# DMA transposes of q and k in three parts, ten x buffers and a new order, in a sliding-window attention with a gated feed-forward stage

## The chip, the core and the metric

The kernel runs on one core of one Trainium2 chip. The metric is device microseconds for one execution of the whole program. Of this kernel four runs are known: 302.01, 302.12, 302.18 and 303.75 us, median 302.15 us. A core has engines that each work through their own list of instructions in order and wait for each other by semaphores: PE (matrix products and transposes through the systolic array), DVE (vector), ACT (scalar functions), POOL (here it makes the masks' distances and issues loads that also convert f32 to bf16) and SP (here it issues stores and DMA transposes).

## The reference

There are 8 batches of 8 heads, 576 positions and 64 values per head. The first half is attention over a window of 128 positions back, with a linear bias per head; the second is a feed-forward stage with h * cos(h) between its two products.

```python
scores = scale * np.matmul(q, k.transpose(0, 1, 3, 2))      # scale = 1/8
bias = slopes[:, None, None] * (-np.abs(rel).astype(np.float32))[None, :, :]
mask = (rel >= 0) & (rel < window)                           # rel = i - j, window = 128
scores = np.where(mask, scores + bias[None], -1000000000.0)
attn = softmax of scores over j
x = (attn @ v), rows (batch, position), columns (head, value)   # 4608 x 512
h = x @ w_in                                                 # 512 -> 2048
out = (h * np.cos(h)) @ w_out                                # 2048 -> 512
```

## The kernel before

**Work.** The 4608 rows of x are 9 chunks of 512. A chunk's feed-forward stage is `moe1` (16 blocks of `w_in`; each block is 4 matmuls at L768, a cosine on ACT at L774 and a multiplication on DVE at L778 that writes g) and `moe2`, the second product (L909; chunk 0 has its own forms at L792 and L853). From chunk 1 on `moe2` computes seven products of half-sized blocks (P1 to P7) from sums of weights and of g; its `read` steps on ACT (L929) and DVE (L933) add them and write one of four output buffers `ob`, which `store` (L954) sends to memory. A buffer can be written again only when its last store has landed.

**Attention.** A batch is nine units: four head pairs for the first 256 positions (G = 0), four for the next 256 (G = 1), and a tail of 64 positions for all heads. For a unit PE computes scores (L538), ACT the exponential (L568), DVE the mask (L592), PE the product with v (L623, L626), DVE the division (`norm`, L664, or for two units at once L679), which writes x into a buffer of `xnat`. x must then be transposed into `xT`. For units that the next chunk needs, PE does it (`x_pe`, `x_pe_two`) and ACT or DVE copies; for others SP issues a DMA transpose (`x_dma`, L753; tails from `xtail`, L748). The buffers of `xnat` are used in turn, `n % NX`, so a `norm` must wait until the transpose that read its buffer NX units earlier has landed.

**q and k.** They are needed with the head's 64 values on partitions. Batches 0 and 1 (`BPE = 2`) are transposed on PE by `qk_transposes` (L481) into two PSUM banks at a time, and copied out by ACT (L498) and DVE (L499). Batches 2 to 7 are loaded by POOL (`load_nat`, L339, five loads each for q and k) into `qnat` and `knat`, two buffers each, and transposed by DMA into `qt` and `kt` (`dma_transposes`): one transfer of the first four blocks of 128 positions (L350) and one of the tail of 64 (L353), with one semaphore for both. Every score group of a batch waits for all of that batch's q and k. Loads of batch 3 wait for batch 2's transposes.

**Order.** The code describes operations with what they read and write (`op`), a modelled length `occ` and delay `lat`. POOL's operations keep the order of the code. For all others the order on each engine, and which of ACT and DVE takes an operation that both could do, come from a table of start times, `STARTS`, that was made beforehand and stands in the file in packed form. `schedule` sorts by it; `emit` turns the dependences into semaphore waits. So the engines' lists are fixed when the program is built, and an instruction whose input is late holds up all that stands behind it on its engine.

Of the kernel before, what the change touches and what calls it, by code (L numbers as in the profile page):

```python
# [14 lines left out]
B, H, S, D = 8, 8, 576, 64  # L15
NPAIR = H // 2
NBLK = 5
# [10 lines left out]


STARTS = (  # L30
    "c-pO24RBP|72cOXa(x5(I4W)~i!PU!n68h_l0Nn)ci$#JvTT>Qh5<sb{46Q06ag_HP0@nHLTijMGE9d;#FQ$-pI~Q%qT-BFY"
    "cW#GD1!*tv9_RN!730;7P7DBy<IjxyHU&ZC42Y0bI-l^obP<++_eaL+;Z(nNjm=Fn{E-hvv26ov#utlbwS5Rz**D4Fw`x*pT"
    "UBV^`+(7ocZasXYy75rdI*~@V_gyWw)jG2H!=pWYA@ZG2>cuRv5@Gp1~`N9uu;Y?k8>az8(mA2LG}y8DnmDmXKv07aJt#!dG"
    "b#T<xzIe5LQZkY(xYtI59Ro!-mSxEWTr8CvgIy<c2?HTnQ!iXs`~y*B9S7z<ffg|CyW=^i*+18UL~@&1aev~36X#RmzN9m|L"
    "h%0hq4uNR*Te9$uty#ng)CCAJ(4T>9B33!wc6NG+o_j|YGbpG$)WnW3t#QL$Tub(~45lmS~VkM;6q-!h#Xs|qVQ?F;LQ&eUp"
    "8dP`6COh6EW2X=jSr<AJSf!WD_3$c9A@paOklWGUCbu)g`n3Kfq;x`WXN7NEo9XHPj%$TXf$2T?3WgK8U-wWc7Ef8`=obc?T"
    "XdRv64G7j?$5+QSH3*~mT#-$tengJO$K#lWTGX>#O}1+GHZkZ>)346i3_dgP8=LJ&>7s7GRwBaQgT*zSE53MEB_DDr9FdU{j"
    "0GLyUkFNcXK9KdhEYTfeHf`XtJC40y$X@F>{5Wr`25iI#`jW$oV?0mv^OM)HOgq?(UWG-nmX$3IpGSee{AEwh;T)tLM6|t2E"
    "?<^rF9<=4>xF(cZWmu4#JYc(1aEe`APoOIExO=~M2<Q+^BAzSI1Rr?tim8eAXGfJHn5U{yu>`?oQfna`Ic1qF8NvYf3s(e1J"
    "DA4)zHOAc-M4Scrk@ldEN6xvebYB{>~Y^`Iq{>5y)cD(<lGW}FpS((2C2b>RuR@c2}eXYiJXwmKaXTl+vl7A+!oY|a=%_)*P"  # L40
    "1HKXG3(v8R+{ny#JW{7TY(&?nyMvD{TR8pHc=?!gxBV@-U7ku8d-gn%-%`Ma16?JZ*8Z&y2Qo{At=e8jL_*xu%105=FM=di@"
    "jnA99e}zUP+)|JRz6G;32H>^<Z&tiLW$^{JkqulP!<FHY1~6R>D^w!|49rxLW=oZAhLw>RNIUyQV5l|^S?>72F(5Tp&ca+RO"
    "TIM9f%Oc$|r_Oq5<DLw`+?>zZ#95XkRjvZL{s1_2gKXI(n4TJCXWtE|Mx_n;IHhIKu-KOmc^PQJU?OD)K9Q;Ot&+;HAAEsw{"
    "~b(%X+8w?`W&tC0X|K$U{kAOS0m19b#g<044~30(y59NS4iaiLd|gED*bkz0bHdWIUPUhZyV;AUs-f#PCRFuo5YHK4sv6LdH"
    "6iPdjP0quU7v>xX_T-dgW@hiCHiqh4%XQ1?Hrouv=hbPFsH7cI_(+8m%!ka%deDKXhpUNwK8$?;V6P;k=S8w%tF9wg(w}O+$"
    "z$Dq_^iHPsQ7Go;6^DyH|CI-o!ynzh!?oTJN00M>oNqItta{zsFyr;t+m1#*cYTQ98VNNA5Q+8OdlQnBROj(ZT9q=A@ne075"
    "M>%QM6sDr5DWGjNez{Vvdu`PXd8Q`&?z!e^5PN-wKg~1HS&NVV(LX{1#t(8>4cJlDlo?9)>F#(%W4ZW@hLIZxJ|oA)cR)Lv3"
    "<F^llvG{Gd_C(Kvb&$rr3E=HH8V<?->O<UkuU$#=l|_aB6=92KI@Q)N-(wu14tXeCo-=OUBt6>7rNeGe8;Ra*w5#<`%&uCKr"
    "eAypX`h9h&EAK~c-U&j$`Y5N-d6N)3D*e6{M_C!r&uRR?d3ZjME7nH7CExOhl&3M=F(SOd##QaFi?4ZrhFeM}Uw2T>+lcM=i"
    "#3)8@$FAy88Q$$!$Kumn`Q!wVC3yM4FG7yKAt{_wq-`bZb;3At!%8Z@ZDn<Q*8C-fG2+Ypcf-E)h$=;uom1q}LC~NV(QFaI#"  # L50
    "crKL`<eP+T#J3kY<K`ogQFi`VvFu>l2gsR|+H7;5*AOelH$&uvQ=5oPL#zr9@Ba(kZ#(i-5j^?*9ctAw*JB>=&7b2A4c$q*e"
    "9|4>FFa8F!Io(I-ukV-zGsZ}rXkI>?Z4Qvo$f7y=jUJe9C>Bm{%BO+u+hGvWTR6Hd=}jx88L$ihjqS;h}EZ{kw*BQgB0;>go"
    "+Z~h$Dp()Ho@T5#Ji8h;))5XtPm+VtErQ@yo{U#f`(Hd;)1)Jn67ZT$K2oHny~YP<4^}%R)lToeTI56?+ji_;qXIDAL5Apy*"
    "Q-9a6x#SRIN`_n}bfJ=lvxhv>BPJi<&vyY{I_B|}vBTw*Sj?OZn{1_eCV=wn7bXp7BqA)=k%WS$}6X<dd2=NX@8_{|JE0cRE"
    "Lgib!=#r6AdZHbQXc%NxK=MLXhTla=X7B1Cjpv-V8?xD-2`U(z1l}8-j7w9XtCyS()y_?pBqM=QP-#O-J%ZWOo<5VztWi#=k"
    "U_H_-lK_Egl3*3&ttpYEp2D^%Qdyme3Zy`{7ML`4p?6R$ZYOYukA>0GN>sZHqjEU^>Oo2rHw|2BP$IOIKDW}^R7(xM3<IoP-"
    "=9FDO{K3o{#DmnI@PPPhQ-T{OF=vD07_Nf9axVndqRQ}v!1Ph0P^mP6lip7XC#H@Xrr)&70i2HVM+m?zQLiedp<&j+O;VYmV"
    "`b%+ScKLXIjs?!$W^bi#+hN>c+_+kE~MM&pTdm|E{QT%KUQ<Z~lRoX3Z;-W}luZb-IYxMb0-Utq!q)(j>=dt<lGVP?>xeNBB"
    "0;p85<B#b%wKfG|<gINokgKw1W*7!0$#hu0aXc_XUm6v^pz;mFgzCFc6FAo4r3n<#Urzs6|Ez6XO8!@Qq@)HL~&#Foc>AE}*"
    "D=KDverp(TBRYj`RJiCqJy9=+60KZdWwhh`^Rg%@xwcuCmKe!nuS?N;@zh)MF5-Fdf<@>SKRUj<k7uqhLnhsOvSE}KmTj^*I"  # L60
    "{P<X*2P*$Fu4UuWLa(cBbK?o@8Hq?RSZY-Y+{k`$nrL)oBa}&1KmsWM6d+Y~234u~juR@BuQIzE7?oGO5!Nlp+qWJ_Gl*qGr"
    "Ah-Lw7z1>Zs}?S*&IRY?C}SvYAya4YTQk;cl|v)hfRIhp&&!n1cNwgFCJVU<op<HU&`N6BGPic29~x?(;kv!y!~eQ7Yu6F9z"
    "I%!_rUk$`Z_xojy7U-?OLhA0j+~U<Hy=+P}RcHA#;wojzpu!MiQAa_iiM9V_lT`_gGh|;!;sXmMZwmqa4IMU%gEI)J!N<F^{"
    "TskXRiAl^Q=E77`j&t)Eb;h$>NQ9H^t>hB4FklOV2P3iV^vBQ3@*drnkU8B`J^iisvIzPw>ii=A&)DQ%kjqsX?EZf)qfbE<v"
    "%t_ZM_D~lVgH`@98Dny#KeK28(mp>4xYc154)kq8c&s>bwMeKY>^#-=2^tM)@jr{zAh6AkhRI92efBiY0E05o{&>Cv5UU>9v"
    "3RJ<n1J6bGDOuSzoGDvW%;5^=P>5~Yp=U?Wm=P9(W)6)zl_+(A%WOV~H4@%F?QUx3_r2imWCu9pPkf&lJ#6$wB!+Pzoldeq&"
    "+iz$H9-$(Pu7LR&a(dk0l(UW"
)


# [150 lines left out]
def bass_alibi_sliding__then__act_gcu_kernel(  # L221
# [8 lines left out]
    with ExitStack() as ctx:  # L230
# [3 lines left out]
        R = Plan(nc, ctx)  # L234
        op = R.op
# [7 lines left out]
        T = {n: sb(f"wsum{n}", [128, HF, 256], F16) for n in (1, 2, 3, 4)}  # L243
        Sg = {n: sb(f"gsum{n}", [128, HF, 256], F16) for n in (1, 2, 4)}
        qB = {"q": sb("qrows", [128, 2, 1152]), "k": sb("krows", [128, 2, 1152])}
        nat = {w_: [sb(f"{w_}nat{i}", [128, NBLK, H, D]) for i in range(2)] for w_ in ("q", "k")}
# [5 lines left out]
        NP = 4  # L252
        P = [sb(f"p{i}", [128, 2, 512]) for i in range(NP)]
        Pt = [sb(f"ptail{i}", [128, 1088]) for i in range(2)]
        NX = 8
        xbuf = sb("xnat", [128, NX, 256])
        xnat = [xbuf[:, i, :] for i in range(NX)]
        xtl = [sb(f"xtail{i}", [64, 512]) for i in range(2)]
# [76 lines left out]
        def load_nat(which, src, b):  # L335
            fns = []
            for t in range(NBLK):
                rows = 128 if t < 4 else 64
                fns.append(lambda e, t=t, rows=rows: e.dma_start(  # L339
                    nat[which][b % 2][0:rows, t, :, :],  # L340
                    src[b, :, 128 * t:128 * t + rows, :].rearrange("h p d -> p h d")))

            op("pool", fns, r=[("tr", which, 0)] if b == 3 else [], w=[("nat", which, b % 2)],
               dma=f"ldn{which}{b % 2}", occ=4400, lat=4500)

        def dma_transposes(b):
            for which in ("q", "k"):
                t = tr[which][b % 2][:, :].rearrange("p (c k t) -> p c k t", c=NBLK, k=NPAIR)
                fns = [
                    lambda e, t=t, which=which: e.dma_start_transpose(  # L350
                        t[:, 0:4, :, :].rearrange("p c k t -> p (c k) t"),
                        nat[which][b % 2][:, 0:4, :, :].rearrange("p c h d -> p (c h d)")),
                    lambda e, t=t, which=which: e.dma_start_transpose(  # L353
                        t[:, 4, :, 0:64],
                        nat[which][b % 2][0:64, 4, :, :].rearrange("p h d -> p (h d)")),
                ]
                op("sp", fns, r=[("nat", which, b % 2)] + ([("ktail", b % 2)] if which == "k" else []),
                   w=[("tr", which, b % 2)], dma=f"tr{which}{b % 2}", occ=2500, lat=4300)

        def load_w_in(u):  # L360
            op("pool", [lambda e: e.dma_start(
# [141 lines left out]
        def tkeys(u):  # L503
            b, _, G = u
            keys = [("tr", w_, b % 2) for w_ in ("q", "k")] + [("ktail", b % 2)]
            if b < BPE:
                keys += [("tr", w_, b % 2, t0 + j0) for w_ in ("q", "k")
                         for t0, _, groups in PIECES[b] if not (G == 0 and t0)
                         for j0, _ in groups]
            return keys  # L510
# [554 lines left out]
        for c in range(NCH):  # L1065
            if c == 0:
                for i in range(NFC):
                    moe1_half(c, i // 8, i % 8, (OB + SB)[i] if i < 6 else (OB + SB)[i % 4])
                for half in range(2):
                    qk_transposes(1, "q", 0, half, SB[2:4])  # L1070
                    qk_transposes(1, "k", 0, half, SB[2:4])
                load_nat("q", q, 2)
                load_nat("k", k, 2)
            else:
                for fc in range(NFC):
                    moe1(c, fc, (UB + SB)[fc % 6] if done < len(every) else
                         (UB + SB)[(16 * c + fc) % 6])
            n = QUOTA[c] if c < len(QUOTA) else 0
            attention(every[done:done + n], c)
            done += n  # L1080
            while next_t < B and done >= 9 * (next_t - 1):
                load_v(next_t)
                if next_t < 4:
                    tail_zero(next_t)
                dma_transposes(next_t)
                next_t += 1
                if next_t < B:
                    load_nat("q", q, next_t)
                    load_nat("k", k, next_t)
            moe2(c)  # L1090
# [29 lines left out]
```

The softmax here doesn't subtract the row's maximum and nothing guards it: scores larger than these inputs give would overflow.

## Time and profile before

| | before |
|---|---|
| median of 4 runs | 302.15 us |
| profiled execution, its own time | 302.12 us |
| its span | 300.4 us |
| granted TensorE clock | 1.00 |
| PE busy | 291.4 us, 97% of the span |
| DVE, ACT, POOL busy | 240.5, 209.6 and 95.0 us |
| L768, first product of a chunk, in the chain | 36% of the span |
| L909, second product, in the chain | 34% of the span |
| DMA traffic | 38.09 MB, mean 127 GB/s |

The span is the time from the first to the last instruction of the program on the core. In a line of groups or of the timeline, PE, DVE, ACT, POOL are the engines, SPq is SP issuing, L followed by a number is the line of the kernel, and `out<-in` gives the buffers. What stands in brackets after a row is the idle time of the engine before it and what ended it; "issue" there means that the profile shows nothing that it waited for. PE's matmuls are pipelined, so the lengths of neighbouring rows overlap.

### The profile page before, as it was taken

Reading aid. Unit: us, or ns where it says so; the run is one execution under the profiler, and the core shown is the slowest. Engines: PE = TensorE matmul, PEld = TensorE weight load, DVE = VectorE, ACT = ScalarE, POOL = GpSimd, SP = SyncE. Lnnn points to the kernel's source line nnn. Section 1 sums busy time; section 2 is a strip of 40 time slices with the busy share of each in tenths; the row PEclk is TensorE's granted clock in tenths of the full one; section 3 lists DMA queues with packets and bytes.
Section 4 is the critical chain, followed back from the end, with each engine's and each line's share of the span. In section 5 each row is a group of like instructions: output and inputs, shape, how many; then the busy total and the mean of one; then the engine's idle time right before and its main releaser. Section 6 shows DMA issues by size and latency. Waiting matters only on the chain.

```text
span 300.4 us, 7105 instructions
## 1 busy us (share of the span) xinstructions
PE 291.4 (97%) x2905; PEld 200.6 (67%) x2925; DVE 240.5 (80%) x478; ACT 209.6 (70%) x300; POOL 95.0 (32%) x122
## 2 busy tenths in 40 slices
PE   7799999999999999999999999999999999999996
PEld 3568746547774578547888886568746855566685
DVE  4587678879978998899988889788978967685871
ACT  6787978398857788588768685778676945644432
POOL 7998230059955702760196004000000000000000
DMA  7999999999999999999999999932304111120033
GB/s 139 180 199 210 206 168 174 139 165 144 188 141 140 173 159 156 144 183 166 174 117 146 136 119 159 170 71 65 98 26 99 44 30 52 37 77 30 0 124 122
DMA packets 148352, 38.09 MB, mean 127 GB/s; under 512 B 133984, under 2 KB 147040, under 8 KB 148320
## 3 DMA queue, kind: packets, MB, share of 16 engines
q0 software_dynamic: 99344, 18.10, 78.0%
q1 hardware_dynamic: 48976, 19.54, 36.2%
q8 instruction: 23, 0.38, 0.5%
q14 instruction: 9, 0.07, 0.1%
HBM read 36.70 MB, written 9.44 MB: 154 GB/s over the span
## 4 chain that ended last, share of the span: by engine, by line
PE 93%; DMA 2%; DVE 1%; issue 1%; POOL 1%; ACT 0%; POOLq 0%; DVEq 0%; ACTq 0%
PE ps L768 36%; PE ps L909 34%; PE ps L792 5%; PE ps L853 5%; PE ps L538 5%; PE ps L623 3%; DMA krows<-in_k_dram 2%; PE ps L626 2%; PE ps L481 1%; PE ps L692 1%; PE ps L528 1%; PE ps L610 1%; PE ps L612 1%; DVE xnat L664 1%; POOL krows L310 0%
## 5 line engine op out<-in xcount | busy, mean ns | idle before, releaser
L768 PE MATMUL ps<-xT,w_inb 128*128 128x512 bf16 (+1 forms) x556 | 125.2, 354 | 0.7
L774 ACT ACTIVATE cos<-ps,halfpi 128x512 f32<-128x512 f32 x128 | 82.3, 686 | 46.3 <-PE ps L768 34.9
L778 DVE TENSOR_TENSOR gT<-ps,cos 128x512 f16<-128x512 f32 x128 | 83.0, 685 | 21.6 <-ACT cos L774 21.1
L768 PEld LDWEIGHTS ps<-xT,w_inb 128*128 128x128 bf16 x576 | 55.2, 98 | 39.7 <-DVE xnat L679 0.8
L568 ACT ACTIVATE p<-ps 128x768 bf16<-128x768 f32 (+1 forms) x64 | 55.6, 917 | 8.5 <-PE ps L538 7.6
L329 POOL DMA_DIRECT2D vp<-in_v_dram x40 | 34.0, 872 | 64.1 <-PE ps L626 50.5
L909 PE MATMUL ps<-wsum,gT 128*128 128x256 f16 x256 | 50.8, 273 | 0.4
L592 DVE TENSOR_TENSOR p<-p,emask 128x512 bf16<-128x512 bf16 (+2 forms) x88 | 39.0, 471 | 3.4 <-ACT p L568 3.0
L909 PE MATMUL ps<-w_outb,gT 128*128 128x256 f16 x256 | 39.7, 273 | 0.1
L909 PE MATMUL ps<-wsum,gsum 128*128 128x256 f16 x256 | 37.2, 273 | 0.1
L339 POOL DMA_DIRECT2D qnat<-in_q_dram x30 | 25.4, 897 | 20.6 <-DMA qt<-qnat 17.1
L909 PEld LDWEIGHTS ps<-wsum,gT 128*128 128x128 f16 x256 | 24.2, 98 | 9.1 <-DVE ob L933 0.8
L909 PEld LDWEIGHTS ps<-w_outb,gT 128*128 128x128 f16 x256 | 24.5, 98 | 8.4 <-ACT ob L929 0.3
L909 PEld LDWEIGHTS ps<-wsum,gsum 128*128 128x128 f16 x256 | 24.7, 98 | 4.6 <-ACT qrows L929 0.2
L339 POOL DMA_DIRECT2D knat<-in_k_dram x30 | 25.6, 927 | 3.3 <-issue 3.3
L909 PE MATMUL ps<-w_outb,gsum 128*128 128x256 f16 x128 | 26.1, 273 | 0.1
L679 DVE TENSOR_TENSOR xnat<-ps,rec 128x512 bf16<-128x512 f32 x28 | 19.3, 690 | 1.3
L929 ACT ACTIVATE qrows<-ps 128x512 f32<-128x512 f32 (+1 forms) x18 | 9.9, 552 | 14.2 <-PE ps L909 14.1
L538 PE MATMUL ps<-qt,kt 64*128 64x128 bf16 (+1 forms) x320 | 18.4, 239 | 0.5 <-issue 0.3
L623 PE MATMUL ps<-vp,p 128*128 128x65 bf16 x256 | 18.0, 193 | 0.8 <-DVE xT L740 0.4
L623 PEld LDWEIGHTS ps<-vp,p 128*128 128x128 bf16 x256 | 15.6, 97 | 3.9 <-issue 1.2
L626 PE MATMUL ps<-vp,p 128*128 128x65 bf16 x192 | 16.9, 193 | 0.0
(81 smaller groups left out, 333.3 us busy)
## 6 DMA issues: line engine op xcount, KB each, us to landing
out_dram<-ob SPq DMA_DIRECT2D x32, 256.0 KB, 4.2
vp<-in_v_dram POOLq DMA_DIRECT2D x32, 128.0 KB, 9.2
qnat<-in_q_dram POOLq DMA_DIRECT2D x24, 128.0 KB, 12.8
knat<-in_k_dram POOLq DMA_DIRECT2D x24, 128.0 KB, 17.3
w_inb<-in_moe_w_in_dram POOLq DMA_DIRECT2D x4, 512.0 KB, 10.8
w_outb<-in_moe_w_out_dram POOLq DMA_DIRECT2D x4, 512.0 KB, 22.2
out_dram<-ob SPq DMA_DIRECT2D x8, 128.0 KB, 1.7
qrows<-in_q_dram POOLq DMA_DIRECT2D x1, 576.0 KB, 15.5
```

Source lines behind the costliest of these rows:

```text
L329: op("pool", [lambda e, t=t, rows=rows: e.dma_start(vp[b % 2][0:rows, t, :, 0:64], v[b, :, 128 * t:128 * t + rows, :].rearrange("h p d -> ...
L339: fns.append(lambda e, t=t, rows=rows: e.dma_start(nat[which][b % 2][0:rows, t, :, :], src[b, :, 128 * t:128 * t + rows, :].rearrange("h p ...
L538: ins = e.matmul(ps[:, banks[x], c0:c1], keys_ap(b, x, pr, kc), query_ap(b, x, pr, qb, 128 * nb), start=not added, stop=True, skip_group_c ...
L568: op("act", lambda e: e.activation(P[i][:, :, 0:hi], src_[:, :, 0:hi], ACTF.Exp, scale=0.125), w=held + [("P", i)], occ=920 if G else 691, ...
L592: op("dve", lambda e, p=p, m=m: e.tensor_tensor(p, p, m, ALU.mult), r=[("P", i), ("EM", h0), ("EM", h1)], w=[("P", i)] if n != 1 else [("P ...
L623: ins = e.matmul(o, P[i][:, x, d0:d0 + 128], V[:, kc, h, 0:65], start=True, stop=not two)
L626: ins = e.matmul(o, P[i][:, x, p0:p0 + 128], V[:, kc - 1, h, 0:65], start=False, stop=True)
L679: op("dve", lambda e: e.tensor_tensor(o, U[:, :, :, 0:64], rv[:, :, :, None].broadcast_to([128, 2, 4, 64]), ALU.mult), r=[("rec", n // 2 % ...
L768: op("pe", lambda e, kc=kc, c0=c0: e.matmul(ps[:, bank, c0:c0 + n], w_in[:, kc, 128 * fc:128 * fc + 128], xT[:, kc, (r0 + c0) % XR:(r0 + c ...
L774: op("act", lambda e: e.activation(cosb[ci][:, :], ps[:, bank, :], ACTF.Sin, bias=halfpi[:, 0:1]), r=["halfpi"], w=[("B", bank), ("cos", c ...
L778: op("dve", lambda e: e.tensor_tensor(gT[gi][:, fc, :], ps[:, bank, :], cosb[ci][:, :], ALU.mult), r=[("cos", ci)], w=[("B", bank), ("g", ...
L909: op("pe", lambda e, t=t, fc=fc, bk=bk: e.matmul(ps[:, bk, 256 * t:256 * t + 256], lhs(fc, t), rhs(fc), start=first and fc == 0 and (last ...
```

## The change

- `NX`, the number of x buffers in `xnat`, goes from 8 to 10.
- `dma_transposes` issues three transfers for each of q and k: blocks 0 and 1, blocks 2 and 3, and the tail, each with a semaphore of its own, in the code's order k before q. For batches 2 to 7 that is 36 DMA transposes in place of 24.
- `tkeys`, the list of what a score group waits for, names parts: a unit with G = 0 needs the first part of q and k, one with G = 1 the second part of q and the first two of k, the tail unit the last of q and the last two of k.
- Loads of batch 3 wait for the second part of batch 2's transposes only.
- The PE transposes of batch 1's q go to the other pair of PSUM banks, those of its k stay.
- The modelled lengths of the transposes change, and the table of start times is a new one: order and choice of engine change throughout. In the new lists ACT and DVE share some copies differently, and on SP the parts of the transposes stand between stores and x transposes.

```diff
-        NX = 8
+        NX = 10
...
-            op("pool", fns, r=[("tr", which, 0)] if b == 3 else [], w=[("nat", which, b % 2)],
+            op("pool", fns, r=[("tr", which, 0, "p", 1)] if b == 3 else [], w=[("nat", which, b % 2)],
                dma=f"ldn{which}{b % 2}", occ=4400, lat=4500)
 
         def dma_transposes(b):
-            for which in ("q", "k"):
-                t = tr[which][b % 2][:, :].rearrange("p (c k t) -> p c k t", c=NBLK, k=NPAIR)
-                fns = [
-                    lambda e, t=t, which=which: e.dma_start_transpose(
-                        t[:, 0:4, :, :].rearrange("p c k t -> p (c k) t"),
-                        nat[which][b % 2][:, 0:4, :, :].rearrange("p c h d -> p (c h d)")),
-                    lambda e, t=t, which=which: e.dma_start_transpose(
-                        t[:, 4, :, 0:64],
-                        nat[which][b % 2][0:64, 4, :, :].rearrange("p h d -> p (h d)")),
-                ]
-                op("sp", fns, r=[("nat", which, b % 2)] + ([("ktail", b % 2)] if which == "k" else []),
-                   w=[("tr", which, b % 2)], dma=f"tr{which}{b % 2}", occ=2500, lat=4300)
+            for part, (c0, c1) in enumerate(((0, 2), (2, 4), (4, 5))):
+                for which in ("k", "q"):
+                    t = tr[which][b % 2][:, :].rearrange("p (c k t) -> p c k t", c=NBLK, k=NPAIR)
+                    src_ = nat[which][b % 2]
+                    if part < 2:
+                        o = t[:, c0:c1, :, :].rearrange("p c k t -> p (c k) t")
+                        i = src_[:, c0:c1, :, :].rearrange("p c h d -> p (c h d)")
+                    else:
+                        o = t[:, 4, :, 0:64]
+                        i = src_[0:64, 4, :, :].rearrange("p h d -> p (h d)")
+                    op("sp", [lambda e, o=o, i=i: e.dma_start_transpose(o, i)],
+                       r=[("nat", which, b % 2)] + ([("ktail", b % 2)] if which == "k" else []),
+                       w=[("tr", which, b % 2, "p", part)], dma=f"tr{which}{b % 2}{part}",
+                       occ=3150 if part < 2 else 1300, lat=1900 if part < 2 else 500)
...
             keys = [("tr", w_, b % 2) for w_ in ("q", "k")] + [("ktail", b % 2)]
+            parts = {"q": (0, 1, 2), "k": (0, 1, 2)}
+            if b >= BPE:
+                parts = {0: {"q": (0,), "k": (0,)}, 1: {"q": (1,), "k": (0, 1)},
+                         None: {"q": (2,), "k": (1, 2)}}[G]
+            keys += [("tr", w_, b % 2, "p", i) for w_ in ("q", "k") for i in parts[w_]]
...
-                    qk_transposes(1, "q", 0, half, SB[2:4])
+                    qk_transposes(1, "q", 0, half, SB[0:2])
                     qk_transposes(1, "k", 0, half, SB[2:4])
```

The lines of `STARTS` are left out of the diff; all of them change.

## The prediction

> **What bounds the kernel now.** I read the page's totals first, then the chain, then idle time by stretch, then the waits of PE, and only then the queue that the change rewrites (SP).
>
> ```profile
> span 300.4 us, 7105 instructions
> PE 291.4 (97%) x2905; PEld 200.6 (67%) x2925; DVE 240.5 (80%) x478; ACT 209.6 (70%) x300; POOL 95.0 (32%) x122
> PE 93%; DMA 2%; DVE 1%; issue 1%; POOL 1%; ACT 0%; POOLq 0%; DVEq 0%; ACTq 0%
> ```
>
> PE is busy for all but 9.0 us, and 93% of the chain is PE. The stretches say where the 9.0 us lie (first column the stretch, second its length, third PE's busy time):
>
> ```profile
> 0.00:5.00 5.00, 3.74 (x9) 1.20 (x9) 1.09 (x7) 2.45 (x5) 3.42 (x12) 1.00 0.52 134
> 5.00:10.00 5.00, 4.17 (x75) 2.77 (x76) 3.13 (x13) 4.17 (x10) 5.00 (x7) 1.00 1.22 164
> 10.00:15.00 5.00, 3.35 (x70) 2.40 (x70) 3.28 (x9) 4.03 (x6) 5.00 (x8) 1.00 1.79 181
> ...
> 30.00:40.00 10.00, 10.00 (x115) 6.82 (x113) 7.32 (x13) 8.68 (x14) 1.57 (x2) 1.00 1.29 204
> 40.00:50.00 10.00, 10.00 (x100) 5.49 (x99) 7.66 (x18) 7.78 (x10) 3.30 (x4) 1.00 2.36 166
> ...
> 175.00:200.00 25.00, 24.48 (x235) 15.17 (x236) 20.91 (x44) 17.61 (x26) 3.32 (x4) 1.00 1.02 141
> ...
> 275.00:300.40 25.40, 22.40 (x179) 17.34 (x179) 14.39 (x25) 9.83 (x19) 0.00 (x0) 1.00 0.22 73
> ```
>
> Up to 25 us PE idles 4.4 us, of which 1.3 us come before its first instruction; from 25 to 275 us it idles 1.6 us in all; the last stretch idles 3.0 us, nearly all of it the last eviction, store and landing. The waits of PE are short and, apart from those at the start, hardly there:
>
> ```profile
> PE ps L481 <- DMA krows<-in_k_dram: 0.7, 1, 0.7
> PE ps L730 <- DVE xnat L664: 0.6, 1, 0.6
> PE ps L623 <- DVE xT L740: 0.4, 1, 0.4
> PE ps L538 <- issue: 0.3, 1, 0.3
> ```
>
> The fourth is the one PE wait that the timeline puts on the transposes of q and k, at 178.4 us. In the timeline (start, length, engine, line, operation):
>
> ```profile
> 178.65 0.51 PE L538 MATMUL ps<-qt,kt 64*128 64x256 bf16 x8 [0.28 <-issue]
> ```
>
> Two more places of the timeline matter below: SP's queue from 120 us, and a row of DVE that needs a store to have landed.
>
> ```profile
> 120.39 4.89 SPq L350 DMA_TRANSPOSE qt<-qnat  x1
> 125.33 1.38 SPq L353 DMA_TRANSPOSE qt<-qnat  x1
> ...
> 130.57 0.61 SPq L954 DMA_DIRECT2D out_dram<-ob  x1
> ```
>
> ```profile
> 139.87 0.69 DVE L933 TENSOR_TENSOR ob<-ps,qrows 128x512 f32<-128x512 f32 x1
> ```
>
> **The change part by part.**
>
> *PE's own work.* Both programs hold the same 2,925 weight loads and matmuls; only their order differs. So the 291.4 us stay. One thing in the order has a price: entering a score group or a PE transpose from other work. Five L909 matmuls start at 200.81 and the score group after them at 201.45: 0.64 us where five steps of 0.109 make 0.545, so 0.10 us per entry. Before has 39 such entries, after 40: **+0.1 us**.
>
> *The start, up to 21 us.* The new order takes the bias and score matmuls of heads pair 2 out of the wait for the last k rows and puts them behind it. Step by step: the k rows land at 10.94 as before (POOL's order is unchanged), transposes run 10.98 to 11.66, bias and scores of pair 3 to 12.37 as before, then those of pair 2 (0.44 and 0.27) to 13.08, so the first L623 group starts at 13.1 against 12.76. Both copies of kt now stand on DVE, 0.87 us each, where ACT took one: 11.78 to 13.4, just in time. ACT then runs the exponentials of pair 3, pair 2 and two groups of 0.97 until 15.95, and the xT copy, two exponentials and another copy that follow reach to 18.5. DVE's masks (0.68 each, a 0.28 copy between) end at 17.9, so the next L623 group starts at 17.95 against 17.84, with 9 of the first L792 matmuls done instead of 11 (2 x 0.109). At the following L623 group DVE has one more mask ahead of the copy that it waits for: 20.7 against 20.39, with 15 L792 matmuls done against 16. That is 0.3 + 0.1: **+0.4 us**. Bounds: −0.6 if the waits of the second and third lines above (0.6 and 0.4) go and nothing replaces them but the 0.4; +1.0 if a further 0.6 us wait of the same kind comes. I take +0.4, since the chain of rows gives it.
>
> *Batch 1's PE transposes in two bank pairs.* They could spare waits for the copies out of one pair (0.87 to 0.88 us a copy). But from 30 to 50 us PE is busy 20.00 of 20.00 us: the L792 and L853 matmuls fill those waits. **0**; if that cover were gone, one copy, +0.9.
>
> *Ten x buffers.* No row of the waits shows DVE waiting for an xT transpose before it writes xnat. **0** directly; it lets the new SP order send x transposes later. A gain needs a wait that isn't there; a loss would be an x transpose that lands late, which belongs to SP's queue below.
>
> *DMA transposes in three parts.* The 12 of L350 (16 blocks, 4.9 to 6.7 us of SP while loads run, 2.1 when they don't) become 24 of 8 blocks; the 12 of L353 (1.3) stay. A half has no row: between an xnat transpose (2 blocks, 1.25) and the whole (6.7). I take half of a whole, 2.6 for the first after a quiet spell (4.89/2), 3.0 behind another. So SP issues 12 more, at least 0 and at most 12 x 1.3 = 16 us, on a queue that PE doesn't read. What it buys: a score group waits for its own parts. The 0.28 us wait at 178.4 is for the tail of batch 6's q, issued at 171.23. In the new order the first halves of q and k of batch 6 go out near 147 and 161; the wait goes: **−0.3 us**. The first group of batch 3 becomes the tighter one: its k half now stands behind the batch 2 tail, whose xtail DVE finishes 0.8 later than the 90.6 of now; 91.9 + 1.25 + 3.0 is issued at 96.2, and with 6.7 us more (the median landing of xT transposes issued between 120 and 175 us) it is there by 103, ahead of the scores at 104.4.
>
> By the Trainium skill ("DMA: Bandwidth & Descriptors", section "Anatomy of one DMA") each DMA carries a fixed cost of about 2.0 us, mostly the receipt of the last write, which speaks against cutting one transfer in two. The smallest transposes here landed in 2.3 us in a quiet stretch (205 to 231 us), so the trace agrees. As an estimate from the page, 12 more would be 24 us, and the sum 324; but receipts overlap, and none of these lies on PE's path, so the sum below holds without it.
>
> *What is late next.* SP now issues, from batch 5's q rows at 120.4 on: q half 2.6, q tail 1.4, q half 3.0, batch 4's k half 3.0, an x transpose 1.3, a store 0.5, and then the store of output buffer 0 of chunk 2 at 132.4, where before it left at 130.57. Stores issued from 126.8 to 141.3 took 6.4, 7.7 and 8.6 us (least, median, most) to land: 138.8 to 141.0, median 140.1. The DVE addition at 139.87 writes that buffer for chunk 3 and must wait for it; behind it on DVE stand sums of g and masks, behind those PE's next group on the bank that it frees. With the shifts above the addition comes due near 140.4. So the margin goes from 1.6 us to 0.3. At the median nothing is lost; at the worst 0.6 us, and 1 us more for each us that SP is later. Bounds 0 and +1.5; **+0.2 us**.
>
> *Sum:* 300.4 + 0.1 + 0.4 − 0.3 + 0.2 = 300.8 us of span. The profiled execution took 302.12 us, 1.7 more than its span and level with the median of 302.15; so 302.5 us.
>
> **The rivals.**
>
> *Slower: the late store at 140 us.* If halves issue at 3.6 us instead of 3.0 behind each other (a whole was 6.68 at 132.5), or the q rows of batch 5 land 1.9 us later, the store lands at 142 or more and DVE, then PE, lose over 1.6 us: 304.0 and up, and the same queue then delays chunk 2's other two stores behind the batch 4 tail (issued near 153.7, due 162.5): 305. For it: SP has almost no free time from 149 to 183. Against it: a pause of SP ahead of 120.4, so that the first half meets an empty queue. It decides from 1.9 us of delay.
>
> *Faster: the start closes up.* If the new order really fills the 3.1 us of waits up to 20.4 us, at best 1.5 to 2 us go: 300.4. For it: these are the only waits worth having. Against it: the k landing at 10.94 is the same, and less work stands in front of it.
>
> *The split does nothing at all:* only 0.28 us ever waited for it; then 302.8, inside the forecast.
>
> **How the numbers follow.** A change under 0.5% (1.5 us, 300.6 to 303.7) can't be told from none here; the four runs alone spread over 1.7. No change: 0.70; slower: 0.22; faster: 0.08. The likeliest is 302.5. The range takes the start's bounds (−1.0 and +0.6 about the sum) below, and above it the store's +1.5 with the start's +0.6: 301.1 to 304.6.
>
> **What would show it.** Right: PE busy 291 to 292 us; the wait at 178.4 gone; a PE wait of 0.7 us or a little more kept before the last k transposes, lengthened to about 1.7; a DVE row that waits for a store near 140 us, if any wait is new. Wrong: any PE wait over 1 us after 25 us, above all at 104, 137 or 140 us; PE's idle time up to 21 us more than 1 us away from 4.4; halves that take SP over 3.4 us each.

## The result, and the profile after

The changed kernel takes 303.30 us (median of 50 runs, 302.78 to 304.79) against 302.11 us for the kernel before (76 runs): a ratio of 1.0038 with a 95% interval of 1.0029 to 1.0047, so 1.2 us slower. Timed once more beside other kernels on one chip (five runs against 23) it took 303.32 us against 301.74, a ratio of 1.0054 (1.0040 to 1.0068), 1.6 us slower. The forecast was 302.5 us in a range of 301.1 to 304.6, with "within 0.5%" as the likeliest case: the first ratio is inside that bound, the second a little outside, with an interval that reaches to both sides of it. Times are medians and ratios come from all runs, so the two need not agree in the last digit. Four of the 50 runs, and some runs of the later kernels, had a granted clock of 0.993 or 0.994 instead of 1.00 and were some 1.5 us longer, which lifts a ratio more than a median; where it matters (the first experiment) the median of the runs at the full clock is given too.

Where a row of the kernel before had line L481, L538, L623, L909, L933 or L954, the changed kernel has L484, L546, L631, L917, L941 or L962. Its totals and its chain of waits, from the page:

```profile
span 301.6 us, 7142 instructions
PE 292.1 (97%) x2905; PEld 200.7 (67%) x2925; DVE 245.3 (81%) x483; ACT 206.7 (69%) x295; POOL 94.9 (31%) x122
...
PE 89%; DVE 5%; DMA 2%; issue 1%; POOL 1%; ACT 1%; POOLq 0%; ACTq 0%
```

PE is still the bound, but DVE now carries 5% of the chain where it had 1%, and PE's busy time has grown by 0.7 us. The stretches (start and end, length, then the busy times of PE, its weight loads, DVE, ACT and POOL, each with its number of instructions, then the granted clock, the share of the DMA engines and GB/s):

```profile
0.00:5.00 5.00, 3.74 (x9) 1.19 (x9) 1.32 (x7) 2.62 (x5) 3.42 (x12) 1.00 0.51 134
5.00:10.00 5.00, 3.71 (x69) 2.86 (x68) 3.13 (x13) 3.50 (x8) 5.00 (x7) 1.00 1.27 169
10.00:15.00 5.00, 4.23 (x80) 2.99 (x80) 3.77 (x10) 4.55 (x7) 5.00 (x8) 1.00 1.82 181
...
30.00:40.00 10.00, 10.00 (x126) 6.98 (x125) 8.37 (x15) 7.18 (x12) 0.00 (x0) 1.00 1.20 200
40.00:50.00 10.00, 9.02 (x81) 4.43 (x80) 7.78 (x19) 6.34 (x9) 8.13 (x10) 1.00 1.27 84
...
175.00:200.00 25.00, 24.89 (x243) 16.10 (x245) 21.09 (x44) 18.68 (x27) 3.31 (x4) 1.00 1.00 121
```

Two of them stand out. From 40 to 50 us PE idles 0.98 us, where before it was busy throughout; and POOL, which in the kernel before was still issuing loads at 28 us, is idle from 17 to 41.9 us (fifth busy time of a row), with 84 GB/s moved from 40 to 50 us (last number) against 166. From 175 to 200 us PE idles 0.1 us against 0.5. The waits of PE:

```profile
PE ps L631 <- issue: 1.0, 1, 1.0
PE ps L484 <- DMA krows<-in_k_dram: 0.9, 1, 0.9
PE ps L631 <- ACT xT L747: 0.6, 1, 0.6
PE ps L484 <- ACT qrows L323: 0.6, 1, 0.6
PE ps L546 <- DVE kt L402: 0.5, 1, 0.5
PE ps L738 <- DVE xnat L672: 0.2, 1, 0.2
...
PE ps L917 <- DVE ob L941: 0.2, 1, 0.2
```

The first has no counterpart before and no releaser. It is found by following what L631 (the product with v) reads, back through POOL to DVE. Three views of the changed kernel's timeline, PE, POOL and DVE:

```profile
47.33 0.25 PE L631 MATMUL ps<-vp,p 128*128 128x65 bf16 x3 [0.98 <-issue]
```

```profile
13.94 2.99 POOL L370 DMA_DIRECT2D w_outb<-in_moe_w_out_dram  x4
41.87 4.20 POOL L330 DMA_DIRECT2D vp<-in_v_dram  x5 [24.94 <-DVE vp L398]
```

```profile
39.98 1.22 DVE L827 TENSOR_TENSOR wsum<-w_outb 128x2048 f16<-128x2048 f16 x1
41.30 0.27 DVE L398 MEMSET vp<- 64x256 uint32 x1
```

In the kernel before, POOL did not wait there:

```profile
13.62 0.27 DVE L395 MEMSET vp<- 64x256 uint32 x1
```

```profile
16.96 4.24 POOL L329 DMA_DIRECT2D vp<-in_v_dram  x5
```

L398 (L395 before) is a memset of 0.27 us that zeroes the unused half of the last block of batch 1's v buffer. The new order puts it at 41.3 us on DVE, behind a sum of weights; before it stood at 13.62 us and cost 0.27 us of DVE there. POOL keeps the order of the code, and its next instruction, the load of batch 1's v, must come after that memset; so POOL stands for 24.94 us, v's second block lands at 47.24 us, and PE waits.

To see where the rest goes, I take for each PE operation its start in the trace, less the summed lengths of all PE operations ahead of it in the list (0.109 us for a half-width matmul, 0.10 us for an entry into scores, and so on). That is how far PE stands behind its bare work. Entries count as work here, so where one order has more of them up to a time, the delay of one and the same instruction is larger than the table shows. The table gives it as the difference to the kernel before, by the time in the trace, for the two kernels and those experiments that the text below comes back to (us):

| time in the trace | changed | memset put back | and P2 first | memset first | split alone | split, waiting for all parts |
|---|---|---|---|---|---|---|
| 31 | −0.16 | +0.09 | −0.11 | −0.31 | −0.26 | −0.58 |
| 44 | −0.28 | −0.03 | −0.23 | −0.43 | −0.26 | −0.58 |
| 48 | +0.86 | −0.03 | −0.24 | −0.43 | −0.26 | −0.58 |
| 106 | +0.90 | +0.01 | −0.14 | −0.39 | −0.27 | −0.58 |
| 109 | +1.24 | +0.35 | −0.14 | −0.06 | −0.27 | −0.58 |
| 161 | +1.71 | +0.81 | +0.21 | +0.40 | −0.37 | −0.68 |
| 186 | +1.17 | +0.28 | −0.32 | −0.13 | −0.74 | −0.41 |
| 246 | +1.51 | +0.61 | +0.01 | +0.20 | −0.73 | −0.41 |
| 292 | +1.17 | +0.28 | −0.32 | −0.13 | −0.76 | −0.43 |

The first row needs a correction. PE's last transposes of batch 0's k start when the k rows land. In the profiled execution of the kernel before that was at 10.98 us, the latest of all the executions profiled here (10.27 to 10.98), in the changed kernel at 10.67; POOL issues that load at 4.7 us in both. Counted from that landing, the changed kernel is 0.15 us later at 31 us (0.31 less the 0.16 of the table), not earlier. One and the same instruction near 25 us comes 0.35 us later: the new order has 14 entries into scores or x transposes up to there, where before has 12, and the table counts those 0.20 us as work.

### The profile page after: what moved, and what is told of

It is laid out like the page before. It is cut to its first block, busy times and chain, and to the rows that moved or that the text cites. A ratio compares the mean times of both kernels' runs of the same rounds, so it can differ in the third digit from the quotient of the medians.

```text
span 301.6 us, 7142 instructions
## 1 busy us (share of the span) xinstructions
PE 292.1 (97%) x2905; PEld 200.7 (67%) x2925; DVE 245.3 (81%) x483; ACT 206.7 (69%) x295; POOL 94.9 (31%) x122
## 4 chain that ended last, share of the span: by engine, by line
PE 89%; DVE 5%; DMA 2%; issue 1%; POOL 1%; ACT 1%; POOLq 0%; ACTq 0%
PE ps L776 35%; PE ps L917 31%; PE ps L861 5%; PE ps L800 5%; PE ps L546 5%; PE ps L631 3%; DMA krows<-in_k_dram 2%; PE ps L634 2%; DVE gT L786 1%; DVE gsum L851 1%; PE ps L700 1%; PE ps L484 1%; PE ps L536 1%; PE ps L620 1%; PE ps L618 1%
## 5 line engine op out<-in xcount | busy, mean ns | idle before, releaser
L330 POOL DMA_DIRECT2D vp<-in_v_dram x40 | 34.0, 889 | 69.3 <-PE ps L634 41.3
L917 PE MATMUL ps<-wsum,gT 128*128 128x256 f16 x256 | 50.3, 273 | 0.2
L917 PE MATMUL ps<-w_outb,gT 128*128 128x256 f16 x256 | 39.3, 273 | 0.1
L917 PE MATMUL ps<-wsum,gsum 128*128 128x256 f16 x256 | 38.2, 273 | 0.2 <-DVE ob L941 0.2
L917 PEld LDWEIGHTS ps<-w_outb,gT 128*128 128x128 f16 x256 | 24.6, 98 | 8.4 <-issue 0.3
L917 PEld LDWEIGHTS ps<-wsum,gT 128*128 128x128 f16 x256 | 23.8, 98 | 8.1 <-issue 0.6
L917 PEld LDWEIGHTS ps<-wsum,gsum 128*128 128x128 f16 x256 | 24.5, 98 | 5.2 <-DVE ob L941 0.4
L917 PE MATMUL ps<-w_outb,gsum 128*128 128x256 f16 x128 | 26.9, 273 | 0.1
L631 PE MATMUL ps<-vp,p 128*128 128x65 bf16 x256 | 18.0, 193 | 1.8 <-issue 1.0
L631 PEld LDWEIGHTS ps<-vp,p 128*128 128x128 bf16 x256 | 15.4, 97 | 5.8 <-issue 2.8
L546 PE MATMUL ps<-qt,kt 64*128 64x128 bf16 (+1 forms) x320 | 18.4, 239 | 0.6 <-DVE kt L402 0.5
```

The source lines that it names most:

```text
L330: op("pool", [lambda e, t=t, rows=rows: e.dma_start(vp[b % 2][0:rows, t, :, 0:64], v[b, :, 128 * t:128 * t + rows, :].rearrange("h p d -> ...
L546: ins = e.matmul(ps[:, banks[x], c0:c1], keys_ap(b, x, pr, kc), query_ap(b, x, pr, qb, 128 * nb), start=not added, stop=True, skip_group_c ...
L631: ins = e.matmul(o, P[i][:, x, d0:d0 + 128], V[:, kc, h, 0:65], start=True, stop=not two)
L917: op("pe", lambda e, t=t, fc=fc, bk=bk: e.matmul(ps[:, bk, 256 * t:256 * t + 256], lhs(fc, t), rhs(fc), start=first and fc == 0 and (last ...
```

## The experiments

All were timed against the kernel before on the same chip. Where a diff shows `o.start`, `schedule` overrides a start time of the table (in units of 25 ns); the kernels that mix the two orders carry a table of their own. Line numbers differ a little between them.

**The memset put back.**

```diff
             o.start = code >> 1
+            if i == 33:            # the memset of batch 1's v buffer
+                o.start = 510      # 12.75 us, as before
```

> The changed kernel with one step of DVE put back: the memset of batch 1's v buffer (L398) stands at its old place near 13 us instead of 41 us. Theory M (the memset holds POOL's loads of v for 24.9 us, and PE then waits 0.98 us for v at 46.35 us): that wait goes, POOL issues v from 17 us, and the time falls by 0.9 us from 303.3 to 302.4, ratio to before 1.001. Rival O (the loss sits in the new order as a whole, and PE would only wait elsewhere for what comes next): the time stays at 303.3. Rival C (the loads of v and of batch 2's q and k now run beside the start's loads again, and the start loses what it had won without them): 302.7, with PE about 0.3 us later at 25 us than in the changed kernel.

302.45 us against 301.67, ratio 1.0040 (1.0021 to 1.0059); the median of the eight runs at the full clock is 302.34 us, 0.67 us above before, where the changed kernel itself stood 1.19 us above in its first comparison and 1.58 in the second. In the timeline POOL no longer stands:

```profile
16.89 4.24 POOL L332 DMA_DIRECT2D vp<-in_v_dram  x5
```

PE's wait at 46 us is gone, and from 48 us to the end PE is 0.89 or 0.90 us ahead of the changed kernel in every row of the table. Theory M holds, and the traces give the size. The start is 0.25 us worse than the changed kernel's at 31 us, as rival C had it, but not for its reason; the eleventh experiment shows which. What rival O wanted to explain is there as well: 0.7 us remain.

**The memset late, in the kernel before.**

```diff
+            if i == 33 or i > 72 and o.eng == ("pool",):
+                o.start = max(o.start, 1632)   # 40.8 us; POOL's later loads stand behind it
```

> The kernel before with that one step alone: the memset behind the first sum of weights near 40.7 us, and POOL's loads from v of batch 1 on behind it. Theory M: v's second block lands near 46.5 to 47 us as in the changed kernel, PE's first product with v of batch 1 comes due at 45.06 us here, so PE waits 1.4 to 1.9 us and the time rises to 303.5 to 304.0, less 0.3 us if the start gains from the loads that are gone. Rival O: 302.1 unchanged, no PE wait over 0.3 us near 45 us.

303.57 us against 301.67, ratio 1.0065 (1.0046 to 1.0085). The timelines of POOL and PE in this kernel:

```profile
40.81 4.20 POOL L331 DMA_DIRECT2D vp<-in_v_dram  x5 [23.77 <-DVE vp L397]
```

```profile
46.00 0.25 PE L625 MATMUL ps<-vp,p 128*128 128x65 bf16 x3 [1.45 <-issue]
```

The same wait comes into the old order by this one step, 1.45 us long since PE gets there earlier; the whole rise is 1.9 us by the median of six runs, of which the profiled one, 302.82 us, is the shortest. Rival O fell.

**The split alone, in the old order.** The parts of `dma_transposes` and `tkeys` of the change, eight x buffers, the old bank pairs, each old transpose's place on SP taken by its three parts in order.

> The kernel before, in its own order, with the DMA transposes in three parts and score groups that wait for their own parts; eight x buffers, the old bank pairs, each old transpose's place on SP taken by its three parts. Theory S (the split spares the waits of the scores at 178.4 and 182.5 us, 0.28 and 0.13 us, and costs nothing on PE's path): 0.3 to 0.5 us less, 301.7. Rival N (something else waits in their place, nothing is gained): 302.1. Rival Q (the longer time of the halves on SP delays stores and x transposes, DVE waits for a buffer): 302.5 or more, with a wait on a store that before does not have.

301.14 us against 301.67, ratio 0.9981 (0.9970 to 0.9992): 0.5 us faster, and the twelve runs lie within 0.62 us where the 29 of the kernel before spread over 1.65. Theory S holds for the first of its two waits. The scores of the first group of batch 6, which waited 0.28 us in the profile before, start without a wait:

```profile
177.92 0.50 PE L538 MATMUL ps<-qt,kt 64*128 64x256 bf16 x8
```

The second, of 0.13 us, stands ahead of a first-product matmul at 181.93 us in this trace too.

**The new order of the start alone.** As the last kernel, but with the changed kernel's order up to a planned 25 us, the memset at its old place.

> The third kernel of this call with the changed kernel's order of all engines up to a planned 25 us (the memset of v at its old place) and the order of before from there. It differs from the third in the start alone. The prediction's step: 0.4 us more than the third. Rival R (read from the two traces, where PE was 0.15 to 0.27 us ahead at 25 to 39 us): 0.2 us less than the third. Rival L (the last k rows landed 0.3 us earlier in that one execution, the order is worth nothing): the same as the third.

301.86 us against 301.14 for the split alone: 0.7 us more (ratio to before 1.0008, 0.9995 to 1.0020). Counted from the landing of the k rows, the same instruction near 25 us comes 0.73 us later, and PE is 0.53 us further behind in the measure of the table, which counts two more entries as work. The step has the sign that was expected and is larger than 0.4 us, with the memset at its old place here; rivals R and L fell. The two traces that R was read from had different landings, and the changed kernel's lacked the memset.

**Split, and the memset in DVE's first idle time.** As the third kernel, with the memset at 1.4 us.

> The kernel before with the transposes in three parts (the third kernel of the first call) and the memset of batch 1's v buffer moved into DVE's idle time at 1.4 to 4.0 us, behind the first memsets. Theory D (at 13.6 us that memset takes 0.27 us of DVE on the way to the first xnat, and PE's transposes wait for it: the changed kernel's trace is 0.25 us further at 17 us than the same kernel with the memset put back): 0.25 us less than with the split alone, so 0.7 to 0.8 us less than before. Rival (the 0.25 us were the landing of the first k rows in those executions): no less than with the split alone, 0.5 us less than before.

301.31 us against 301.74, ratio 0.9991 (0.9978 to 1.0004): no better than the split alone. In the old order those 0.27 us of DVE do not reach PE, so theory D failed there.

**The changed kernel once more.** No edit.

> The changed kernel once more, beside the others on one chip. With the memset put back it stood 0.78 us above before by the medians of one chip, the changed kernel 1.19 us above it by those of others, where the traces show 0.89 us between the two. Theory M (0.9 us for the wait at 46 us less 0.25 us that the free DVE wins at 13.6 us, so 0.6 us in all): 1.2 to 1.4 us above before here. Rival (the loads' late start costs nothing on the whole): 0.8 us above before.

303.32 us against 301.74: 1.58 us above before, more than either expected. In this trace the wait for v costs 0.84 us, in the first one 1.14: PE reached it about as early in both, but v's second block landed at 46.85 us here and at 47.24 there.

**The new order from 95 us on.** The third kernel with ten x buffers and the changed kernel's order from a planned 95 us.

> The kernel before with the transposes in three parts, ten x buffers, and the changed kernel's order of all engines from a planned 95 us on. Theory T (the new order is tighter for DVE: from 104 us on PE's products with v, its x transposes and the second product each wait 0.1 to 0.3 us for masks, xnat and a read by DVE): 0.75 us more than with the split in the old order, so 0.2 to 0.3 us above before. Rival (the loss that the memset leaves is all in the start): 0.5 us below before, as with the split alone.

301.78 us against 301.74, ratio 1.0006 (0.9991 to 1.0021), so 0.6 us above the split alone by the medians and 0.3 us by the traces once the k landings are allowed for. The step at 108 us is not in this kernel, though P2's matmuls stand there in the new order; the smaller ones after 115 us are. Theory T is right in kind and its size too large by that step, of which the ninth experiment says more.

**One store later.**

```diff
+            if i == 984:           # store of output buffer 0, chunk 2
+                o.start = 5150     # behind the k half of batch 5
```

> The changed kernel with one store later: output buffer 0 of chunk 2 leaves SP behind the k half of batch 5, near 136.2 us instead of 131.86. The prediction's rival: the store lands 8.4 us after its issue as in the changed kernel, at 144.6, the DVE addition due at 141.48 waits 3.1 us for it, and PE loses most of that: 2 to 3 us above the changed kernel. Rival (landing is shorter or PE is covered by the next chunk's first product): under 0.5 us above it. With the median landing of all stores of the changed kernel, 2.8 us, DVE would wait nothing and the time would stay.

303.19 us (six runs, 302.46 to 303.71) against 303.32 for the changed kernel on the same chip, so the 2 to 3 us that the prediction's slower rival asks for did not come. The profiled execution, the longest of the six, shows that rival's mechanism all the same. SP and DVE in its timeline:

```profile
133.88 0.59 SPq L964 DMA_DIRECT2D out_dram<-ob  x1
```

```profile
141.86 0.69 DVE L943 TENSOR_TENSOR ob<-ps,qrows 128x512 f32<-128x512 f32 x1 [0.80 <-DMA out_dram<-ob]
```

The k half took 1.42 us of SP, not 3, so the store left 2.0 us later than in the changed kernel's first trace, not 4.3, and landed at 141.84. DVE waits 0.80 us for it, and PE then stands 0.79 us further back than in the changed kernel on this chip: once the margin is used up, the delay reaches PE in full. That most executions kept the margin is read from the medians alone; no other execution was profiled.

**P2 first.** The memset put back, and in chunk 2's second product five matmuls of product P6 moved behind the last of P2.

```diff
+            if 985 <= i <= 989:    # five matmuls of P6
+                o.start = 4249     # behind 982, the last of P2
```

> The changed kernel with the memset put back to 13 us, and one thing more: in chunk 2's second product the first five matmuls of product P6 stand behind the last of P2 instead of between them. Theory B (in the new order P2's bank is read too late: 10 matmuls of 0.11 us lie between P2's last matmul and the next product on that bank, where before had 16, and DVE's read takes 0.69 us and its signals; PE waits at 108.2 us): PE is 0.3 us further from 109 us on than without this edit, its wait for DVE's read at 108.2 us is gone, and the time is 0.3 us less, 302.1 on a chip where before has 301.7. Rival (the 0.3 us come from the masks and P2's bank is not what binds): no change at 109 us.

301.89 us against 301.78, ratio 1.0002 (0.9988 to 1.0017): 0.1 us above before, where 0.4 was expected. With the memset put back and P2's matmuls between those of P6, PE's timeline had

```profile
106.93 1.25 PE L919 MATMUL ps<-wsum,gsum 128*128 128x256 f16 x10
108.34 0.83 PE L919 MATMUL ps<-wsum,gsum 128*128 128x256 f16 x6 [0.16 <-DVE ob L943]
```

and with P2 first it has

```profile
104.80 1.59 PE L921 MATMUL ps<-w_outb,gT 128*128 128x256 f16 x13
106.23 2.56 PE L921 MATMUL ps<-wsum,gsum 128*128 128x256 f16 x22
```

The step of 0.34 us at 106 to 109 us, which every execution with the whole new order shows alike (0.34, 0.34 and 0.33 us in the table), is gone, so it comes from this place: P2's sum stands in a PSUM bank that the next product needs, and DVE must read it first. But theory B's count does not explain it. Ten matmuls lie between in the new order and twelve before (not the 16 of the expectation), and the seventh experiment has the same ten and no wait. What differs is DVE's read. With the memset put back, and in the seventh experiment, DVE's timeline has

```profile
107.59 0.69 DVE L943 TENSOR_TENSOR ob<-ps,qrows 128x512 f32<-128x512 f32 x1 [0.37 <-ACT p L578]
```

```profile
106.75 0.69 DVE L934 TENSOR_TENSOR ob<-ps,qrows 128x512 f32<-128x512 f32 x1
```

The second read starts 0.41 us after the start of P2's last matmul (106.34), as in the kernel before; the first 0.77 us after it (106.82). The releaser that the profile names, an exponential on ACT, is no input of the read. With P2 first there is cover for either. Why the read idles 0.37 us in the one order and not in the other stays open.

**Ten x buffers alone.** `NX = 10` in the kernel before.

> The kernel before with ten x buffers and nothing else. The prediction's step: 0, as no wait in the trace is for an x transpose that a buffer's next writer needs. Rival (DVE's rewriting of a buffer waits for SP's transposes without showing it): 0.2 to 0.5 us less.

301.84 us against 301.78, ratio 1.0013 (0.9996 to 1.0030): no gain, and no change clear of the noise. Whether the new order needs the two further buffers was not tried.

**The changed kernel with the memset first.** The override of the first experiment with a start of 48 (1.2 us).

> The changed kernel with the memset of batch 1's v buffer in DVE's idle time at 1.6 to 4.0 us. Theory D (in the new order, where DVE runs without a gap from 13.2 us on, the 0.27 us at 13.5 us cost PE 0.37 us by 25 us, read from where PE stood at 16 and at 25 us in the changed kernel and in that with the memset put back; in the old order they cost nothing, as two runs show): PE's wait at 46 us is gone and the start keeps what it wins without the memset, 0.9 to 1.0 us less than the changed kernel, 302.3 where it has 303.3. Rival (the start wins by v's late loads, not by the free DVE): 0.6 us less than the changed kernel, as with the memset put back.

302.03 us against 301.78, ratio 1.0017 (1.0004 to 1.0029), so 0.25 us above before where the changed kernel stood 1.19 or 1.58 above. Two rows of DVE's and PE's timelines:

```profile
1.50 0.27 DVE L400 MEMSET vp<- 64x256 uint32 x1
```

```profile
14.44 0.28 PE L740 MATMUL ps<-ident,xnat 128*128 128x128 bf16 x2
```

With the memset at 13.5 us that last row was

```profile
14.85 0.28 PE L740 MATMUL ps<-ident,xnat 128*128 128x128 bf16 x2 [0.36 <-DVE xnat L674]
```

v is loaded early here, and the start is as fast as the changed kernel's: counted from the k landing, PE at 31 us is in the table's measure 0.14 to 0.16 us behind before in all four executions whose new order has no memset there, this one with its early loads among them, and 0.52 to 0.53 us in all three that have it. So it is the free DVE that wins 0.37 us, not the loads that stay away. Theory D holds for the new order; in the old one the memset is worth 0.1 us at most, as the second and the fifth experiment show when counted in the same way (−0.05 and +0.07).

**Split, waiting for all parts.** The third kernel with the three lines taken out of `tkeys` that name the parts of a group.

```diff
-            if b >= BPE:
-                parts = {0: {"q": (0,), "k": (0,)}, 1: {"q": (1,), "k": (0, 1)},
-                         None: {"q": (2,), "k": (1, 2)}}[G]
```

> The kernel before with the transposes in three parts as in the third kernel of the first call, but every score group waits for all parts of its batch's q and k again. Theory W (the gain of 0.5 us comes from groups that wait for their own parts alone; in the old kernel the tail of batch 6's q lands within some tenths of the scores' due time, 178.56 us against 178.37 in its profile, so that some executions wait and others do not): most of the gain goes, 0 to 0.2 us below before, and the runs spread over more than 1 us like those of before. Rival Z (the smaller transfers pass SP and the DMA engines faster, and what a group waits for does not matter): 0.5 us below before, with runs as close together as with the split (0.6 us).

301.68 us against 301.51, ratio 1.0009 (0.9995 to 1.0024), with eleven runs spread over 1.25 us and a twelfth at 303.48. Theory W holds: the gain is gone. PE's timeline shows the wait back, and with its releaser:

```profile
178.24 0.51 PE L535 MATMUL ps<-qt,kt 64*128 64x256 bf16 x8 [0.55 <-DMA qt<-qnat]
```

The wait is longer than the 0.28 us before because PE came earlier: this start was 0.58 us ahead. So the landing near 178 us is a floor, and a part of what this execution had won before it was lost there, as the table's last column shows (−0.68 at 161 us, −0.41 at 186). The landing itself moves between executions: the tail of batch 6's q was there at 177.99 us here, at 178.56 in the kernel before and at 177.90 with ten x buffers alone, whose trace has no such wait. That executions which come early lose their lead there fits a gain of the split above the 0.28 us that one trace showed; their share was not measured.

## Why the prediction was right or wrong

The time came out inside the range and the case was the likeliest one, but the sum of 300.8 us of span was 0.8 us short of 301.6, and 1.1 us short at the k landing of the kernel before. That it stayed inside is in part luck: the largest loss was in no term of the sum, and the room above the sum had been made for a store that then cost nothing. Step by step:

- *What it left out: the memset.* "The k rows land at 10.94 as before (POOL's order is unchanged)" was true of POOL's order and was then taken to hold for its times. The changed DVE order was followed step by step up to 21 us; that a memset had left that stretch was not noticed, nor who waits for it. Its absence won 0.37 us at the start, and its late place costs 0.84 to 1.14 us at 46 us (shown by putting it back, and by moving it in the kernel before). The prediction named "any PE wait over 1 us after 25 us" as a sign that it was wrong, and looked for it at 104, 137 and 140 us; it came at 46, with 0.98.
- *PE's own work and its entries, +0.1.* The entries were counted, the waits under 0.2 us that do not show in the list of waits were not. The new order loses 0.34 us at 108 us by a bank that DVE reads late (the place is shown, why the read is late is open), some 0.47 us more from 109 to 161 us and 0.34 between 186 and 246, and wins back 0.34 after that. The rows after 115 us are entries into products with v that come 0.12 to 0.19 us late, with masks or x just finished by DVE; that DVE is the cause of each was read from the traces and not tried one by one.
- *The start, +0.4.* Right, row by row. The rows of the last group that the step names, before and after:

```profile
20.39 0.20 PE L623 MATMUL ps<-vp,p 128*128 128x65 bf16 x1 [0.39 <-DVE xT L740]
```

```profile
20.33 0.19 PE L631 MATMUL ps<-vp,p 128*128 128x65 bf16 x1 [0.60 <-ACT xT L747]
```

With the 0.31 us by which the k rows came earlier, the three groups start at 13.08, 18.03 and 20.64 us, where the prediction had 13.1, 17.95 and 20.7, and with 15 matmuls done against 16 as it said: 0.25 + 0.1, so +0.35 us. What it did not know is that this start stands without the memset: with it the order costs 0.73 us on the same instruction near 25 us, and the memset's absence gives 0.37 back.
- *Batch 1's bank pairs, 0.* PE was busy for 10.00 of 10.00 us from 30 to 40 us; nothing was lost there. It was not tried alone.
- *Ten x buffers, 0.* Confirmed alone.
- *The split, −0.3.* Mechanism right, size too low: −0.5 us alone, since the wait for the tail of batch 6's q also took away what executions had won earlier. In the changed kernel's trace PE catches up 0.54 us between 161 and 186 us. The fixed cost of about 2.0 us for each DMA that the Trainium skill states ("DMA: Bandwidth & Descriptors", section "Anatomy of one DMA", which describes DMAs that POOL issues, while SP issues these) would have made twelve more transfers a loss if it added up; the 0.5 us of gain show that it did not, PE waiting for none of the further landings. The first half of batch 3's k, which the prediction had there by 103 us, landed at 102.0.
- *Halves of 2.6 and 3.0 us on SP.* In the changed kernel a half took 1.24 to 4.20 us of SP, and four of the 24 passed the 3.4 us that was named as wrong; yet nothing came of it, as the next point shows.
- *The late store, +0.2.* It did not bind. It left SP at 131.86 us (132.4 predicted, though the terms that were named add up to 132.2) and landed at 140.26 (140.1 predicted), but the addition on DVE came due at 141.48, 1.1 us later than predicted, because the lost time at 46 us had moved everything behind it:

```profile
140.78 0.68 DVE L851 TENSOR_TENSOR gsum<-gT,gsum 128x1024 f16<-128x1024 f16 x1
141.48 0.69 DVE L941 TENSOR_TENSOR ob<-ps,qrows 128x512 f32<-128x512 f32 x1
```

The agreement of 131.86 with 132.4 is luck. With the memset put back, the only difference, batch 5's q rows landed at 106.2 us in place of 120.7, SP started their halves at 116.14 in place of 120.75, and the store left at 127.09 and landed at 132.17, 8.4 us before the addition at 140.58. So in the new order the store is late only because the memset holds POOL's loads. The slower rival's mechanism is real all the same: 2.0 us more on SP made 0.80 us of it. It was not what made this kernel slower.

Of the signs that were named, PE's busy time (292.1 us) and its idle time up to 21 us (4.3 us) came out as said or within 0.1 us. The wait before the last k transposes was 0.9 us, 1.2 at the landing of the kernel before, and not 1.7; the wait for ACT's q rows ahead of it grew from 0.3 to 0.6 us. A few sums of the prediction do not come out as written and change nothing: 24 us on the sum make 324.8 and not 324, 0.8 on 90.6 make 91.4 and not 91.9, and by its own words the range begins at 301.5 and not at 301.1.

Of the two further rivals, "the start closes up" was wrong (the start came 0.35 us later), and "the split does nothing at all" fell with the third and the last experiment.

The best kernel that came out is the old order with the transposes in three parts: 0.9981 (0.9970 to 0.9992) of the time before.

## What to carry to other kernels

When an order is made anew, list every operation that changed its place by more than a few microseconds, the smallest included, and ask of each who waits for it and what stands behind that waiter: here 0.27 us of DVE held a queue of loads for 25 us. Compare starts from the landing that releases them, not from the clock, since the same code got its rows between 10.27 and 10.98 us. A wait for a landing that is fixed elsewhere can swallow what was won ahead of it, as 0.27 of 0.68 us were here; take it away before judging any earlier gain. A queue that looks late may be late for an earlier cause: here the store of 132 us hung on the memset of 41 us.

## What was not expected of the hardware

- Two halves of a DMA transpose cost SP together about what the whole costs while the queue is busy. In the kernel before the twelve transfers of 16 blocks took 60.0 us of SP, 1.86 to 6.68 each; the same places with halves (the split alone) took 62.2 us in twelve pairs. Within a pair the first was mostly short and the second long, 1.36 and 5.04 us in the worst case against 6.51 for the whole: on the busy queue SP's time went by the blocks and not by the number of transfers. In the quiet stretch near 190 us a half took 1.30 to 1.34 us against 1.86 and 2.11 for a whole, so two halves cost 0.5 to 0.8 us more there.
- The landing of the first loads varied by 0.7 us between executions (10.27 to 10.98 us for the first transpose of the k rows). Counted from that landing, executions with the same order of the start stood within 0.08 us of each other at 31 us, most of them within 0.02.
